# A hand-laid instruction order is replaced by another, and half of the last batch's inverse transform takes its other form

## The chip, the cores and the metric

The kernel runs on one core of a Trainium2 chip. The metric is the device time of one execution in microseconds (us); the kernel before takes 386.0 us, the median of three runs (385.96 to 386.59).

Engine names: PE is TensorE (matrix products), DVE is VectorE, ACT is ScalarE, POOL is GpSimd, SP is SyncE, which here only issues DMAs. Each engine works through its own queue in order; an instruction that waits holds everything behind it.

## The reference, cut to what matters

```python
# attention: batch 4, 8 heads, 768 rows, 64 channels a head, 16 clusters
q_assign = argmax(q_n @ c_n.T);  k_assign = argmax(k_n @ c_n.T)   # per row
mask   = q_assign[:, None] == k_assign[None, :]
attn   = softmax(where(mask, (q @ k.T) / 8, -1e9)) @ v
# then, per batch, on the 768 x 512 matrix x of all heads:
proj = x @ w_proj;  x1, x2, x3 = thirds of proj
conv = irfft(rfft(x2, axis=rows) * rfft(filter, axis=rows))
out  = (x1 * conv * x3) @ w_out
```

## The kernel before

**Attention.** Two heads make a pair; there are 16 pairs, four to a batch. For pair `p` (all names below carry the pair's number):

- four (or eight half) loads bring q and k into the tile `raw`, two loads bring v into `vraw`. There are five `raw` slots (a pair takes two) and three `vraw` slots.
- `tr`: q and k are transposed into `qkT`, for pairs 0 to 2 by PE and a copy, from pair 3 on by two DVE block transposes (L828).
- `cast`: four bf16 copies of it into `aug`, on POOL or ACT.
- `sim`: PE multiplies by the centroids; then `oh`, a chain of DVE steps (L862 to L876) makes the one-hot assignment, and one more step (L900 on ACT, L902 on DVE) scales it. Eight small DMAs, the mask DMAs (L909, 12 KB each, on SP's queue), put it into extra rows of `aug`, so that the scores' product itself carries the mask.
- six steps `sk`, each with `S` (PE, scores into PSUM), `E` (ACT, the exponential of 128x1536 elements into `pb`, L938 or L944), `PV` (PE, into the PSUM tile `outs`, L954), and `acc` (DVE, the running sum of the `pb`, L965).
- `den` (PE) sums `acc` over rows, and a chain follows: an ACT copy (L996), a DMA `dd` to DRAM, a DMA back (`dn`), a DVE reciprocal (L1002), a DMA `dr` out, and two DMAs `rb` that bring it back broadcast. ACT copies `outs` to `osb` (L976); there are two `osb` slots. DVE's step `x` (L1030) multiplies `osb` by `rb` and frees the `osb` slot. PSUM has one `outs`: the next pair's first `PV` waits for this pair's `osb` copy.

**PSUM.** Eight banks: 0 to 2 for scores, 3 and 4 for `outs`, 5 to 7 for everything else. Up to pair 3 a second set of scores may use banks 5 to 7.

**The second part** (`hyena`, one batch at a time, spread among the attention of the next batch): `u` (PE, the x2 projection, split into sum and difference of the halves by DVE), `F` (PE, the forward transform; DVE multiplies by the filter's spectrum `hm`), `G` (PE, x1 and x3, multiplied into the tile x13), `I` (PE, the inverse transform, then times x13 into `y2`), `o` (PE, the product with w_out, a copy, and the store). The letters `I3.0` to `I3.3` are the four channel groups of the last batch. The tables of the transform are made at the start: angles (`ang`), six Sin activations (`sin`), `inv`, and the filter's spectrum (`f`, from the loads `fl`).

**The inverse has two forms.** The direct one: two PE operations, each six products for one half of the rows, and DVE multiplies each half by x13 straight from PSUM (L1119). The butterfly: one PE operation makes an even and an odd part, a copy `od` (ACT or DVE) brings the odd part out of PSUM, DVE adds and subtracts (L1141), and one product with x13 (L1143, DVE or POOL) gives `y2`. Before, the last batch takes the direct form in all four groups, the others the butterfly.

**The order.** `Plan` holds 1564 operations with their dependences; `ORDER` is a written-out list of their numbers in the order in which they are emitted, and so fixes each engine's queue; a letter chooses the engine where two can do it (a: ACT, d: DVE, p: POOL). `Plan.told` follows the list. While it emits, `Plan` keeps a clock of its own, with `LAG` for the time from an operation's end to the release of those that wait for it; that clock decides only which free buffer or PSUM bank a value takes.

Of the kernel before, what the change touches and what calls it, by code (L numbers as in the profile page):

```python
# [29 lines left out]
DIRECT = (3,)  # L30
# [9 lines left out]
0 192 1 9 8 77 47 193 49 78 10 11 263 12 13 79d 14 15 16 17 87p 3 80p 4 5 48 6 7 18 19 35 36 37 38 39 40 41 42 43  # L40
44 45 20 25 26 23 24 55 56a 53 54a 51 52a 46 21 22 61 83d 32 31 88d 30 264 50 84d 29 59a 60a 28 27 57a 58a 34 194
195a 33 198 199a 62 63 64 65 66 67 68 70d 73 75 69 71 72d 76d 196 197a 204 74a 203a 150 151 153 157 200a 104 106
105 103 158 154 201a 255 189 205 89 90d 206 207 208 183 185 182 188 253 186 107 85 209 81 210 202d 211 212d 161 152
162 156 86d 160 164 269 265 267 266a 270a 165 216 184 213 220 187 126 219 259 256 215 108 217 214 260 218 166 155
169 82a 268a 168 170 93 273a 91 95 94 274a 96 92 159 275 272p 2 99 98 163 173 167 171 276 277 278 279 280 281 282
271p 335 221 97 334 283d 111 109 110d 174 340 222 112a 172 224 225 341 342 343 344 345 346 227 228 229 223 232 226
113 233 114a 339a 230 338p 337p 336p 236 237 240 234 241 284 287 285 288 127 291 257 290 289 258 286 254 347 231
235 500 501 124 175 125 329 191 330 176 328 562 324 331 239 128 295 238 292 296 293 348a 327 325 559 354 351 352
355 353 298 242 299 244 506 507 177 508 509 129 243 245 294 311 300 303 304 510 302 511 512 306 513 312 297 504p
130 505p 503p 502p 307 301 308 131 133a 138 139a 349 178 356 493 350 190 261 326 364 365 514a 132a 305 144 180 246  # L50
179 262 310 145a 146a 566 565 181 309 360 361 315 571 357 316 358 567p 572 573 574 575 576 363 577 367 494 491 490
520 517 626 247 492 516 317 522 313 141 372 314 373 569a 359 368 100 570p 140a 369 318 497 496 495 558 515 248 578
319 579a 568a 518 521 249 519 320 586 561 362 366 376 322 321 580 555 587 556 584 557 377 147 370 148a 534 535 374
115 371 375 631 630 379 523 636 142a 524 381 526 382 634p 527 378 134 560 383 637 638 639 323 640 641 136 529 642
380 530 525 528 632a 531 542 135a 633a 543 101 635p 384 333 585 583 533 385 695 696 537 643 119 532 332 581 582 251
538 536 701 539 116a 591 700p 592 540 117 588 702 541 703 386 622 250 625 252 704 387 388 389 589 118a 644a 544 546
595 120a 547 545 596 705 706 594 707 402 400 691 690 564 624 687 685 590 401a 598 403 708 652 688 686 599 143a 600
593 390 650 621 649 404 602 603 597 137a 391a 604 646 651 689 692 620 645 623 548 627 549 395 392 396a 697p 698a
699p 607 601 397 606 394 861 862 608 709a 398 393 399 605 867 648 647 563 716 865p 864p 149a 866a 863p 656 415 868
869 416 657 715 1215 710 499 498 711 855 857 714 712 917 417 870 418 550 611 419 927 871 653 654 612 659 872 918  # L60
551 856 916 613 614 552 553 437 609 610 438 420 660 661 655 405 406 668 446 658 873 628 629 713 669 664 447 665 407
662 926 874 663 615 408 672 667 932 933 409 717 858 666 424 934 554 671 930p 673 875a 928a 421 725 425 726 929a 426
670 412 718 410 674 413 427 411 935 931p 719 721 675 676 422 720 722 677 851 616 880 852 883 876 921 922 881 853
617 854 678 729 723 920 877 879 882 730 414 428 936 724 992 423 937 991 938 429a 733 734 727 450 451 997 737 731
448 735 878 1050 982 618 1212 981 1052 679 1051 859 919 1213 983 1053 431 728 430 939 998 449 732 619 995a 738 996a
940a 903 439 452 435 946 942 440 736 680 993p 904 994a 740 884 885 739 433 741 887 434 886 432p 888 742 891 1214
941 948 860 923 1056 944 947 681 693 743 744 892 436 453 999 890 1057 894 745 694 683 943 746 1000 747 945 682 889
459 461 895 460 896 454 893 899 455a 900 462 898 1001 902 457 1002 897 463 901 956 1062 1060p 464 957 749 1063 684
1064 456 1003 458d 907 949 908 950 905 465 906 952 1059a 953 987 748 985 1049 988 750 466 1004 1005a 1065 1066 467
955 102 1061p 123a 468a 1058a 469 951 758 960 954 961 756 757a 958 909 470 1067 759 760 471p 964 965 986 984 1222  # L70
1047 1223 910 1013 1046 1009 1012 1010 1048 962 1006 1011 1007 1008 798 799 753 968 441 959 911 963 969 966 1025
912 442a 443 967 444 1068 1226a 1026 751 752a 755 754 1069 970 1014 1228 972 445p 1015 971 973 1070a 1229 1230 1231
1232 1233 1283 914 1284 1071 1073 974 1077 1281 975 763 761 762a 1017 765 764 484 1016 1018 485a 486 925 807 768
# [12 lines left out]
489 1365 1118a 1366 1411a 1413 1112 1119 1113d 1331 1121 1120 1368 802 1369 1333 803d 805 804 1122 1372 1114 1332
1334 1367 1115 1371 1123a 1116 1373 806p 1416 1273 1417 1274 1419 1415 1275 848 1124 1126 849a 850 1418 1376 1125
1377 1412 1414 1370 1375 1379 1129 1380 842 1130 843a 1374 1127 1181 1128 1131 1381 1384 1378 1183 1385 1182 1420
1132 1421 1383 1134 1382 1435 1386 844 1335 1336 1276 1133 1388 1436 1135 1337 1136 1389 1387 1139 1423 1424 1137
1140 1422 1427 1138 1426 1141 1428 1425 1155 1156 1431 1429 833 1432 1390 1338 1339 1391 1392 1184 1393 1394 1430  # L90
1434 1438 1340 1395 1439 1187 1433 834a 1440 1442 836 837a 835 838 1341 1396 1185 1186 1188 1189 1437 1190a 1191
1192 1193d 1168 845 1444 1445 1446 1447 1448 1449 839 1441 1172 1174 846a 1450 1169 1443 1451 1173 1175 1466 1170
1171 1176 1177a 1179 1178 1180d 1469 1467 1161 1462 1452 1470 1159 1468a 1160 1163 1472 1162 1471 1164a 1166 1165
1157 1158 1167d 1453 1455 1459 1463 1456 1460 1142 1146 1454a 1458 840a 1461a 1464 1147 1143 1457 1465 1150 1514
1144 1148 1473 1475 1151a 841 847 1152 1145 1153 1149 1490 1494 1518 1520 1154p 1197 1491a 1515a 1495a 1519a 1198a
1516 1517a 1476 1474 1477 1199 1483 1484 1485 1501 1200 1486 1487 1201a 1503 1206 1488 1207a 1489a 1521a 1480 1481
1478 1479 1482 1202 1507 1505 1492 1508a 1502a 1203 1504a 1204a 1506d 1509d 1208 1194 1512 1510 1497 1195a 1493a
# [321 lines left out]
def kernel(  # L421
# [39 lines left out]
    op = P.op  # L461
# [573 lines left out]
    def hyena(b, d0, d1):  # L1035
# [181 lines left out]
```

## Time and profile before

| | |
|---|---|
| median of three runs | 386.0 us (385.96 to 386.59) |
| the profiled execution's own time | 386.6 us |
| its span, first to last instruction | 384.8 us |
| mean granted TensorE clock | 0.988 |
| busy: PE, DVE, ACT, POOL | 364.8, 332.2, 254.0, 58.4 us |
| PE's instructions | 3335 matmuls, all recorded |

Between the span and the execution's own time lie 1.8 us outside the program's instructions. The engines run at the same time, so the busy times do not add up; an engine's idle time costs nothing unless the end of the program waits for it.

A row of the table by stretches reads: from:to and length in us, then busy us and number of instructions of PE, PE's weight loads, DVE, ACT and POOL, then the granted clock, the DMA engines' share and GB/s. A row of the chain reads: start, length, and what ran or was waited for. SPq and DVEq are the sequencers that issue.

### The profile page before, as it was taken

What the parts mean: (1) busy time and instruction counts of PE and PEld (TensorE: products, weight loads), DVE (VectorE), ACT (ScalarE), POOL (GpSimd) and SP (SyncE); (2) the same over time, 40 slices, a digit from 0 to 9 for tenths busy, and PEclk for the clock granted to TensorE, in tenths of its full rate; (3) what the DMA queues carried; (4) which work ended last, traced back from release to release, by engine and by line L of the source; (5) the groups of instructions that cost most, each with busy time, mean ns of one, the idle gap of its engine ahead of it and who ended that gap; (6) DMA issues with size and microseconds to landing.
All of it is one profiled execution on the core that took longest, in us unless ns stands there. A gap on an engine that the chain in (4) does not pass through costs nothing.

```text
span 384.8 us, 8428 instructions
## 1 busy us (share of the span) xinstructions
PE 364.8 (95%) x3335; PEld 188.9 (49%) x3335; DVE 332.2 (86%) x428; ACT 254.0 (66%) x305; POOL 58.4 (15%) x74
## 2 busy tenths in 40 slices
PE   7689897997999999999999999999999999999994
PEld 3243444453444554455444545545454545556662
DVE  7898989796898899799888999998977979887771
ACT  3989985886688676785867764887856555242512
POOL 4005171211202030204013040020101000001000
PEclk9989999999899999999999999999999999999998
DMA  9979594938684664755921435342312003010205
GB/s 179 197 93 170 89 166 86 162 63 139 141 120 81 121 109 85 121 100 112 129 36 40 113 55 119 87 119 46 99 36 75 31 24 119 0 57 29 86 28 191
DMA packets 132289, 37.08 MB, mean 96 GB/s; under 512 B 123485, under 2 KB 125977, under 8 KB 132249
## 3 DMA queue, kind: packets, MB, share of 16 engines
q1 hardware_dynamic: 131000, 34.41, 45.9%
q0 software_dynamic: 1104, 2.10, 3.3%
q8 instruction: 26, 0.43, 0.5%
q14 instruction: 15, 0.11, 0.1%
q10 hardware_dynamic: 144, 0.03, 0.0%
HBM read 30.66 MB, written 6.48 MB: 97 GB/s over the span
## 4 chain that ended last, share of the span: by engine, by line
PE 77%; DVE 7%; DMA 6%; SPq 6%; issue 1%; ACT 1%; DVEq 0%; POOL 0%; POOLq 0%; ACTq 0%
PE outs L954 25%; PE bank L479 22%; PE scores L479 18%; PE outs L479 3%; SPq L909 3%; DMA k<-in_moe_filter_fft_dram 3%; PE bank L986 2%; SPq L541 2%; PE bank L859 2%; PE bank L992 2%; DMA rb<-dr 1%; DMA raw<-in_k_dram 1%; PE bank L745 1%; DVE acc L965 1%; ACT pb L938 1%
## 5 line engine op out<-in xcount | busy, mean ns | idle before, releaser
L938 ACT ACTIVATE pb<-scores 128x1536 f32<-128x1536 f32 x91 | 132.3, 1454 | 56.4 <-PE scores L479 54.2
L954 PE MATMUL outs<-pb,vraw 128*64 128x512 f32 (+1 forms) x768 | 142.9, 494 | 2.3 <-ACT osb L976 2.3
L965 DVE TENSOR_TENSOR acc<-acc,pb 128x1536 f32<-128x1536 f32 x52 | 91.6, 1761 | 2.8 <-ACT pb L938 1.8
L954 PEld LDWEIGHTS outs<-pb,vraw 128*64 128x64 f32 x768 | 55.2, 138 | 71.7 <-issue 59.8
L479 PE MATMUL scores<-aug,aug 128*64 128x256 bf16 (+2 forms) x728 | 76.7, 331 | 7.6 <-ACT pb L938 4.6
L479 PEld LDWEIGHTS <-aug 128*64 128x64 bf16 (+2 forms) x768 | 43.8, 111 | 41.5 <-issue 18.2
L468 POOL CAST aug<-qkT 64x768 bf16<-64x768 f32 x30 | 37.3, 1248 | 163.0 <-PE scores L479 83.1
L479 PE MATMUL bank<-xT,wpj 128*64 128x384 bf16 x384 | 38.1, 326 | 0.0
L479 PEld LDWEIGHTS <-wpj 128*64 128x64 bf16 x512 | 28.9, 110 | 16.2 <-issue 1.2
L1143 POOL TENSOR_TENSOR k<-yy,x 128x768 bf16<-128x768 f32 x7 | 13.0, 1861 | 126.8 <-DVE x L1100 56.6
L479 PEld LDWEIGHTS <-k 128*64 128x64 bf16 (+1 forms) x480 | 23.6, 109 | 17.3 <-issue 4.0
L965 DVE TENSOR_TENSOR acc<-pb,pb 128x1536 f32<-128x1536 f32 x16 | 29.1, 1820 | 0.4 <-ACT pb L938 0.2
L466 ACT CAST aug<-qkT 64x768 bf16<-64x768 f32 x33 | 27.2, 828 | 1.3 <-PE scores L479 0.8
L828 DVE STREAM_TRANSPOSE qkT<-raw 128x768 f32<-128x768 f32 x26 | 24.4, 958 | 2.3 <-DMA rb<-dr 1.7
L1070 DVE TENSOR_TENSOR tm<-bank,hm 128x1024 f32<-128x1024 f32 x18 | 21.6, 1213 | 3.6 <-PE bank L745 2.4
L479 PE MATMUL bank<-wpj,xT 128*64 128x512 bf16 x160 | 20.3, 380 | 0.0
L1030 DVE SCALAR_TENSOR_TENSOR xT<-osb,rb 128x768 bf16<-128x768 f32 x16 | 16.7, 1048 | 3.7 <-DMA rb<-dr 3.4
L479 PE MATMUL bank<-wout,k 128*64 128x512 bf16 x136 | 17.4, 379 | 0.0
L466 ACT COPY os<-bank 128x512 f32<-128x512 f32 x15 | 8.8, 584 | 12.7 <-PE bank L479 11.8
L976 ACT COPY osb<-outs 128x769 f32<-128x769 f32 x16 | 12.8, 798 | 6.0 <-PE outs L954 3.3
L1060 DVE TENSOR_TENSOR k<-bank,us 128x512 bf16<-128x512 f32 x18 | 11.7, 684 | 5.3 <-PE bank L479 2.7
L479 PEld LDWEIGHTS <-xT 128*64 128x64 bf16 x192 | 10.7, 110 | 9.7 <-issue 1.6
(176 smaller groups left out, 408.0 us busy)
## 6 DMA issues: line engine op xcount, KB each, us to landing
vraw<-in_v_dram SPq DMA_DIRECT2D x32, 192.0 KB
rb<-dr SPq DMA_DIRECT2D x30, 192.0 KB
out_dram<-os SPq DMA_DIRECT2D x21, 256.0 KB
raw<-in_q_dram SPq DMA_DIRECT2D x52, 96.0 KB
raw<-in_k_dram SPq DMA_DIRECT2D x52, 96.0 KB
aug<-ohT SPq DMA_DIRECT2D x120, 12.0 KB
k<-in_moe_filter_fft_dram SPq DMA_DIRECT2D x4, 384.0 KB
wpj<-in_moe_w_proj_dram POOLq DMA_DIRECT2D x4, 384.0 KB, 5.0
```

Source lines behind the costliest of these rows:

```text
L466: nc.scalar.copy(o, i)
L468: eng[e].tensor_copy(o, i)
L479: nc.tensor.matmul(out[64 * c:64 * c + 64], lhsT[:, 64 * c:64 * c + 64], rhs, **k)
L828: op("DVE", 0.98, lambda e, j=j: nc.vector.transpose(qkT.t[:, j], raws[p, j].t.rearrange("p t h d -> p (t h d)")), r=[raws[p, j]], w=[(qkT ...
L938: nc.scalar.activation(pb.t[:, :, :S], sps.t.rearrange("p (a b) -> p a b", a=2), Act.Exp, scale=0.125)
L954: nc.tensor.matmul(o.t[64 * hp:64 * hp + 64, lo:hi], vv.t[:, hp, sk], pb.t[:, hp, lo:hi], start=(sk == 0), stop=(sk == NT - 1))
L965: nc.vector.tensor_tensor(acc.t, a, pb.t[:, :, :S], op=Alu.add)
L976: op("ACT", 0.82, lambda e: nc.scalar.copy(osb.t, o.t[:, :S + 1]), r=[o], w=[osb], due=step(i) + 5.0)
L1030: op("DVE", 1.01, lambda e: V.scalar_tensor_tensor(xT.t, osb.t[:, :S], osb.t[:, S:S + 1], rb.t, op0=Alu.add, op1=Alu.mult), r=[osb, rb], w ...
L1060: op("DVE", 0.69, lambda e, m=m, e_=e_, alu=alu, ps=ps, us=us: V.tensor_tensor(uv2()[:, e_, m], ps.t, us.t, op=alu), r=[ps, us], w=[(uv, ( ...
L1070: op("DVE", 1.2, lambda e, i=i, cs=cs, ps=ps, tm=tms[cs]: V.tensor_tensor(tm.t, ps.t.unsqueeze(1).to_broadcast([128, 2, DM]), hm.t[:, i, c ...
L1143: op(("DVE", "POOL"), (0.95, 2.4), lambda e, dt=dt, yt=yt, x13=x13: eng[e].tensor_tensor(y2v()[:, dt], yt(), x13.t.rearrange("p a b -> p ( ...
```

## The change

Four edits:

```diff
-DIRECT = (3,)
+DIRECT = ((3, 2), (3, 3))
...
-    LAG = {"PE": 0.26, "ACT": 0.08, "DVE": 0.08, "POOL": 0.1, "SP": 1.4, "ACTQ": 2.0}
+    LAG = {"PE": 0.26, "ACT": 0.08, "DVE": 0.08, "POOL": 0.1, "SP": 1.8, "ACTQ": 2.0}
...
-            if b in DIRECT:
+            if (b, dt) in DIRECT:
...
-                op("PE", 0.215 * (k1 - k0), f, r=[(y2, (kt, x)) for kt in range(k0, k1) for x in range(1 + (b in DIRECT))] + [wout], w=[ps],
+                op("PE", 0.215 * (k1 - k0), f, r=[(y2, (kt, x)) for kt in range(k0, k1) for x in range(1 + ((b, kt) in DIRECT))] + [wout], w=[ps],
```

and the whole of `ORDER` (1564 entries before, 1566 after) is replaced by a new list:

```diff
-0 192 1 9 8 77 47 193 49 78 10 11 263 12 13 79d 14 15 16 17 87p 3 80p 4 5 48 6 7 18 19 35 36 37 38 39 40 41 42 43
...
-1548 1553 1557 1549 1558d 1550d 1554a 1555 1551 1559
+23 25 26 0 264 24 1 9 35 36 37 38 39 40 41 42 43 44 45 55 46 8 77 78 29 30 31 32 3 2 48 28 27 33 34 10 50 87d 11 12
...
+1547 1548a 1549 1542 1543 1544a 1545 1559 1560d 1561
```

Groups I3.0 and I3.1 take the butterfly, I3.2 and I3.3 keep the direct form. PE's queue has 423 operations for 425, DVE's 423 for 421, ACT's 286 for 291, POOL's 62 for 55, SP's 371 in both. `LAG` for SP goes from 1.4 to 1.8; no instruction waits for it, it only moves the planner's own clock.

The lists in words, at the places that the prediction uses ("place" is the number in that engine's queue, counted from 0):

| queue | before | after |
|---|---|---|
| SP, first mask DMA of pair 1, 2, 3 | places 25, 40, 66 | 21, 48, 65 |
| SP, last mask DMA of pair 1, 2, 3 | 39, 50, 75 | 41, 61, 79 |
| SP, loads of pairs 4 to 6 issued before pair 2's first mask DMA | 5 | 13 |
| pair 3's last one-hot step (`oh3/#5`) | ACT, behind a cast and four `E` of pairs 1 and 2 | DVE, right behind its transpose |
| SP, the two loads of v3 | 56 and 76 | 88 and 93 |
| SP, the two loads of v4 | 77 and 82 | 62 and 76 |
| DVE, `x0`, `x1`, `x2`, `x3` | 98, 133, 118, 135 | 94, 112, 132, 140 |
| SP, `rb` DMAs of pair 1 | 124 and 127 | 106 and 108 |
| ACT, the six `sin` | behind S0's last `E` | between the last two `E` of pair 0 |
| PE, ahead of the first `u` | 33 `S`, 30 `PV`, 8 `sim`, 6 `f` and the rest | 35 `S`, 33 `PV`, 9 `sim`, 5 `f` and the rest |
| four of the last batch's products x1 times x3 | DVE 4 | POOL 3, DVE 1 |
| last PE operation, its copy | `o3.2` second part; two DVE copies in a row | `o3.4` second part; one DVE copy |

Between the fixed places the new list also swaps casts (ACT 33 to 30, POOL 30 to 31, DVE 1 to 3), three steps of the angles to POOL, and the order of the six steps inside a pair.

More of the change, by code (lines that the diff above doesn't have):

```diff
@@ L45 @@
[L45 to L49, printed above, removed]
@@ L100 @@
-1548 1553 1557 1549 1558d 1550d 1554a 1555 1551 1559
+23 25 26 0 264 24 1 9 35 36 37 38 39 40 41 42 43 44 45 55 46 8 77 78 29 30 31 32 3 2 48 28 27 33 34 10 50 87d 11 12
+13 14 15 16 193 192 88p 17 18 49 19 56a 51 52a 53 54a 58a 60a 57a 20 89 90d 263 21 22 61 59d 62 63 64 65 66 67 68
+73 196 197a 198 199a 194 195a 204 202a 69 71 70d 74d 75 72a 76a 161 162 153 154 103 105 106 183 104 203a 157 150
+151 79p 4 83p 5 6 182 186 189 205 200d 206 130 84p 80p 7 207 208 209 210 211 85 212d 201d 81 156 107 158 218 259
@@ new lines @@
+292 295 238 242 296 293 243 244 299 245 509 566 510 511 300 565 512 298 513 302 294 311 297 349 559 496 355 353 126
+350 178 356 352 622 261 354 128 180 351 179 312 620 557 491 621 246 492 303 304 514a 301 357 307 308 305 309 306
+181 360 310 129 495 190 522 517 494 247 191 558 493 518 516 490 358 567p 571 572 248 249 573 515 623 521 562 520
+313 361 568a 314 364 365 117 315 118a 569a 359 570a 316 368 363 574 367 575 631 317 250 519 251 369 576 630 371 577
+556 555 560 318 362 372 373 366 376 377 370 131 523 374 636 375 578 379 252 634a 132a 524 526 133a 579a 527 378 380
@@ new lines @@
+381 637 638 639 640 319 641 529 642 643 530 531 525 119 534 134 528 633p 632p 100 101 635p 382 120a 535 542 141 532
+644a 543 142a 538 539 581 586 561 582 585 583 580 584 320 383 332 533 695 696 651 587 627 384 322 321 625 647 537
+536 699p 385 386 624 701 702 541 591 138 540 700a 135a 592 588 140a 698a 589 333 626 652 388 387 697p 98 703 136
+704 323 861 705 706 862 707 594 544 545 546 599 144 590 600 547 595 596 146a 145a 593 867 603 597 604 708 389 650
+649 548 645 868 395 397 396a 869 870 598 399 607 608 139a 687 648 564 855 549 646 688 690 691 686 692 689 709a 712
@@ new lines @@
+1002 1064 1284 748 981 1222 749 907 905 964 908 906 467 465 951 468a 965 750 1003 1065 466 470 1066 1283 909 910
+986 911 1004 1005a 912 1010 1053 1047 1006 1007 469 1067 955 758 751 752a 956 957 756 954 471p 757a 1013 1009 1011
+1008 1012 1048 1051 960 1223 759 760 961 1068 959 958 807 1228 968 969 962 761 762a 963 1229 1069 1070d 1230 1014
+1077 1076 914 1015 808 966 809 1017 970 967 1231 810 1232 1233 1234 441 1225p 1226p 1227p 1224a 1018 442a 972 444
+1235 443 763 1074 1046 971 1021 1022 445p 753 1016 765 1050 1049 1287 764 754 1020 1024 1025 973 1026 1052 1071 755
@@ new lines @@
+1214 483 813 1100 777 1097 780 1343 814 1102 781 1248 1247 782 1249 783 1252 815 122a 1346a 816a 1253 1101 1041
+1342 784 817 818 1250 1103 1348 1256 1104 1349 1251 1255 785 478 1254 1257 1347a 1344p 1345a 786 1042 1398 819p 484
+1260 796 1258 1105 1106 1107 797 1350 485a 1261 1307 1043 1044 1306 1305 1259 1351 1263 1352 1302 1309 1055 1054
+1108 1110 1109 1264 1265 479a 1262 789 1317 787 790a 792 1045 788 791 1318 1402p 793p 1397 820 1266 1310 800 1353
+801 1268 1267 821 1311 1269 1403 486 1354 1355 1404 1405 1111 1356a 1313 1314 802 472 1312 803a 1406 1407 805 804
@@ new lines @@
+1276 1133 1136 837a 1424 1386 1388 1387 1389 1426 1337 1427 1422 1428 1139 1185 1183 1431 1186 838 1390 1338 1391
+1432 1140 1430 1434 1181 1168 1182 1425 1435 1137 1429 1184 1138 1392 1436 1169 1141 1438 1339 1340 1393 1395 1394
+1439 1440 1442 1433 1189 845 1187 1190a 846a 847 1172 839 840a 841 1444 1192 1341 1191 1445 1396 1446 1188 1447
+1448 1157 1437 848 1449 1193d 1441 1174 1155 1170 1173 849a 850 1156 1443 1450 1451 1175 1176 1171 833 842 1158
+1452 1459 1159 1460 1462 1177a 1178 1179 1180d 1161 1463 834a 1160 1461a 1162 1465 1464 1163 1455 1469 1453 1466
@@ new lines @@
+1456 1470 1142 1467 1164a 843a 1454a 835 1165 1166 1167d 1458 1457 1468a 1143 1471 1144 1145 1472 844 1150 1146
+1151a 1148 1147 1494 1475 1473 1153 1149 1152 1516 1154p 1520 1492 1490 1203 1495a 1204a 1517a 1521a 1476 1474 1477
+1478 1479 1480 1488 1206 1504 1518 1508 1481 1482 1491d 1207a 1493a 1489a 1205 1208 1485 1519d 1486 1483 1484 1487
+1506 1522 1523a 1209 1194 1502 1195a 1503a 1496p 1497 1524p 1509d 1507d 1505d 1210a 1498a 1499 1500 1501d 1525 1527
+1511 1531 1533 1529 1535 1510p 1512a 1526 1528 1513 1211 1196 1200 1514 1532d 1534d 1515d 1540 1536a 1530a 1538
```

80 lines of the change are left out of this document (26 added, 54 removed).

## The prediction

> **What bounds the kernel now.** The first part of the page is read first, then busy time by stretches, because a share over the whole span mixes stages.
>
> ```profile
> span 384.8 us, 8428 instructions
> PE 364.8 (95%) x3335; PEld 188.9 (49%) x3335; DVE 332.2 (86%) x428; ACT 254.0 (66%) x305; POOL 58.4 (15%) x74
> ```
> ```profile
> 0.00:24.00 24.00, 16.18 (x101) 7.97 (x103) 20.41 (x60) 17.34 (x23) 4.67 (x25) 0.93 1.21 174
> 24.00:64.00 40.00, 37.95 (x319) 18.82 (x315) 36.33 (x42) 34.73 (x46) 14.56 (x18) 1.00 0.71 119
> 64.00:72.00 8.00, 5.86 (x54) 3.23 (x58) 5.60 (x6) 5.25 (x8) 0.69 (x1) 1.00 0.95 170
> 72.00:88.00 16.00, 15.66 (x135) 7.89 (x131) 14.97 (x17) 13.08 (x15) 4.51 (x6) 1.00 0.61 89
> 88.00:96.00 8.00, 5.55 (x48) 2.88 (x42) 5.13 (x8) 4.95 (x6) 0.15 (x1) 0.99 0.92 149
> 96.00:104.00 8.00, 7.92 (x55) 3.32 (x52) 6.82 (x8) 5.31 (x6) 1.86 (x3) 0.79 0.55 122
> 104.00:376.00 272.00, 271.91 (x2610) 143.06 (x2608) 241.62 (x289) 171.63 (x203) 31.96 (x23) 1.00 0.37 78
> 360.00:376.00 16.00, 16.00 (x188) 10.48 (x186) 12.36 (x19) 4.42 (x9) 0.00 (x0) 1.00 0.10 35
> 376.00:384.80 8.80, 3.71 (x36) 1.71 (x30) 1.29 (x2) 1.68 (x4) 0.00 (x0) 0.87 0.56 209
> ```
>
> The first busy column is PE. From 104 to 376 us it has work in 271.91 of 272 us at the full clock: there a shorter wait elsewhere buys nothing, and only less PE work counts. Before 104 us it idles 7.82 + 2.05 + 2.14 + 0.34 + 2.45 + 0.08 = 14.9 us, and one stretch runs at a granted clock of 0.79. A microsecond gained there reaches the end undiminished, if DVE (241.62 of 272) keeps up. So the waits are next, first PE's and DVE's, then those of SP's queue, and the chain of work with them.
>
> ```profile
> PE scores L479 <- DMA aug<-ohT: 2.1, 1, 2.1
> PE outs L954 <- ACT osb L976: 2.3, 1, 2.3
> ...
> SPq L909 <- ACT ohT L900: 22.8, 6, 6.3
> SPq L909 <- DVE inv L468: 5.2, 1, 5.2
> ```
> ```profile
> 64.02 1.98 DMA aug<-ohT
> ...
> 86.73 5.71 DMA rb<-dr
> 92.53 1.03 DVE xT L1030
> 93.64 0.81 ACT osb L976
> 94.49 4.07 PE outs L954 x16
> 303.00 1.29 PE outs L954 x8
> ```
> ```profile
> 66.14 0.84 PE L479 MATMUL scores<-aug,aug 80*64 80x512 bf16 x8 [2.15 <-DMA aug<-ohT]
> ```
>
> Three losses can be seen. (a) `S3` stands 2.15 us to 66.14, until the last mask DMA of pair 3 (issued 64.02) has landed. (b) `PV4#0` stands 2.34 us to 94.49: `osb3` had no slot, `x2` frees one, and its `rb` took 5.71 us to land. `x2` is ahead of `x1` on DVE, so neither of the two slots was free. (c) The 16 matrix products behind that wait last 4.07 us; eight take 1.29 us elsewhere, so 4.07 - 2 x 1.29 = 1.49 us goes to the half clock. Together 5.98 us.
>
> **The change part by part: the start.** The loss at (a) has two causes in the old queues.
>
> ```profile
> 43.94 0.57 DVE L876 STREAM_TRANSPOSE ohT<-oh 128x384 bf16<-128x384 bf16 x1
> 52.75 0.71 ACT L900 ACTIVATE ohT<-ohT,mk 128x384 bf16<-128x384 bf16 x1
> ```
> ```profile
> L909 SPq DMA_DIRECT2D aug<-ohT x120: 507/580/1824, 23.1 to 297.7; - x120
> ```
>
> Pair 3's one-hot tile is transposed at 43.94 + 0.57 = 44.51, but its last step runs on ACT at 52.75 to 53.46, 9 us later. And SP stood 5.2 us at place 40, pair 2's first mask, in front of loads that wait for nothing. After, the last step is on DVE right behind the transpose, and 13 loads instead of 5 come ahead of pair 2's masks. Pair 3's last mask moves from place 75 to 79: four more issues of 0.58 us (2.3 us) against 5.2 us not stood, so it is issued at 64.02 + 2.3 - 5.2 = 61.1 by this rough count, at 59.1 when I lay the queue out instruction by instruction with the trace's durations. With 1.98 us to land it is there between 61.1 and 63.1. PE, laid out likewise, reaches `S3` at 61.2; in the old order it was there at 63.99. The wait left is 0 to 1.9 us; I take 0.2, by the finer of the two countings.
>
> At (b), `x1` moves from DVE place 133 to 112 and `x2` from 118 to 132, and with them `rb` of pair 1 goes to SP places 106 and 108. Place 108 was issued at 86.73 before; without the 5.2 us stand that is 81.5. Plus 5.71, 1.03 and 0.81 us, `PV4#0` can start at 89.1, or at 86.3 by the finer laying, where the mask stands and the landings of the long chain of small DMAs fall more favourably. PE gets there between 86.3 (laid) and 90.0 (92.15 less the 2.15 of (a)). The wait left is 0 to 2.8 us; I take 0.8. With that, (c) does not come back; with 2.8 us it would, and cost 1.49 again.
>
> Start-up: 5.98 - 0.2 - 0.8 = 5.0 us gained. Ends: 6.6 us, where the laying puts the first `u` ahead; and 5.98 - 2.8 - 1.49 = 1.7 us, or lower still if DVE decides (rival 2). The reason for caution is DVE: from 24 to 104 us it is busy 36.33 + 5.60 + 14.97 + 5.13 + 6.82 = 68.9 of 80 us. To come 5 us earlier with the same work, its idle time there must shrink from 11.1 to about 6 us.
>
> ```profile
> L965 DVE TENSOR_TENSOR acc<-pb,pb x16: 1744/1750/2379, 23.1 to 314.9; 128x1536 f32<-128x1536 f32 x16
> L468 POOL CAST aug<-qkT x30: 816/825/2397, 29.5 to 262.0; 64x768 bf16<-64x768 f32 x30
> ```
>
> The casts moved from ACT (33 to 30) to DVE (1 to 3) and POOL, and the three angle steps moved to POOL, lie in this stretch too; ACT idled more than DVE in the later part of it, and POOL's 14.56 of 40 us has room. I cost them at nothing; without cover the two casts are about 1.7 us of DVE, by the usual 0.825 us of POOL's, which is inside the gap between 5.0 and 6.6.
>
> [...] The trace has a wait of 2.15 us at 64 with clock 1.00 behind it, and one of 2.34 us at 92 with 0.79 behind it: the shorter shows no dip, the longer does. [...]
>
> **The butterfly in `I3.0` and `I3.1`.**
>
> ```profile
> 110.74 1.73 PE bank L479 x16
> ...
> 188.29 1.10 PE bank L479 x16
> ...
> 369.77 1.95 PE outs L479 x24
> ```
> ```profile
> L1141 DVE TENSOR_TENSOR yy<-bank,od 128x384 f32<-128x384 f32 x20 | 10.8, 551 | 2.4 <-ACT od L466 2.3
> L1143 DVE TENSOR_TENSOR k<-yy,x 128x768 bf16<-128x768 f32 x5 | 4.8, 955 | 0.1
> L1119 DVE TENSOR_TENSOR k<-outs,x 128x384 bf16<-128x384 f32 x4 | 2.1, 554 | 0.6 <-PE outs L479 0.6
> L466 ACT COPY od<-bank 128x384 f32<-128x384 f32 x8 | 3.8, 476 | 2.7 <-PE bank L479 2.6
> L1104 DVE TENSOR_TENSOR x<-x,raw 128x768 f32<-128x768 f32 x4 | 3.8, 954 | 0.2
> L1143 POOL TENSOR_TENSOR k<-yy,x 128x768 bf16<-128x768 f32 x7 | 13.0, 1861 | 126.8 <-DVE x L1100 56.6
> ```
>
> The direct form's two PE operations are the 1.95 us (last row), a butterfly's one is 1.10 (the row before; the first is the first `u`): PE saves 2 x (1.95 - 1.10) = 1.7 us in a stretch where it is busy 16.00 of 16.00. Against that, DVE loses 4 products of 0.554 and gains 4 of 0.551 and 2 of 0.955: +1.9 us; ACT gets 2 copies of 0.476. Between 360 and 376 us DVE is busy 12.36 and ACT 4.42 of 16, and two of four products x1 x3 more than pay for it (3 go to POOL, -2.9 us on DVE; POOL has none at all then). The latency grows: copy, two steps, product, 0.48 + 2 x 0.55 + 0.96 = 2.5 us in place of 0.55. What follows is `I3.2` and `I3.3` in the direct form, 3.9 us of PE work, so the output product that reads `y2` does not wait. Without that cover the cost is up to 2 x (2.5 - 0.55) = 3.9 us, and a product on POOL comes 1.86 - 0.95 = 0.9 us later; so this part is -1.7, with ends -1.7 and +2.2 (all of the cover gone). I take -1.7, by the 3.6 us that DVE idles in 16.
>
> **The end.**
>
> ```profile
> 379.33 0.38 PE L479 MATMUL scores<-wout,k 128*64 128x512 bf16 x2
> 379.59 0.69 DVE L468 COPY os<-outs 128x512 f32<-128x512 f32 x1 [5.32 <-PE outs L479]
> 380.20 0.68 DVE L468 COPY os<-scores 128x512 f32<-128x512 f32 x1
> 380.91 0.81 SPq L1159 DMA_DIRECT2D out_dram<-os  x2
> ```
>
> PE ends at 379.71, the span at 384.8. After, one DVE copy instead of two in a row follows the last PE operation: it starts about 0.1 us behind it instead of 0.49 (-0.4), and one issue instead of two stands before the store (0.81 for two, -0.3 to -0.4). Taken: -0.7, ends 0 and -0.8.
>
> `LAG`: no instruction waits for it. It can change which slot or bank a value takes, and that costs something only where a slot is reused sooner: 0 taken, and any cost falls under rivals 1 to 3.
>
> **Sum.** Span 384.8 - 5.0 - 1.7 - 0.7 = 377.4; with the 1.8 us outside it 379.2, against 386.6 for the profiled execution. That one is the highest of the runs shown (385.96 to 386.59), 0.6 over their median of 386.0. I forecast 379.0 for the median, between 378.6 and 379.2.
>
> **Rivals.**
>
> 1. v3 comes late. Its second load moves from SP place 76 to 93, behind the pair 1 step that waits for a DMA to land. My laying issues it at 67.5 and has `PV3#0` at 71; a landing like `rb`'s 5.71 gives 73.2, a wait of 2.2 us in place of (a), and by (c) a dip of 1.49 with it: 379.0 + 2.2 + 1.5 = 382.7. For it: 0.95 of the DMA engines' time is taken from 64 to 72, and 0.92 from 88 to 96. Against: fewer bytes should be ahead of it, as the masks now stand apart from the loads. Chance 0.13.
>
> 2. DVE becomes the bound, and the new start brings nothing: only butterfly and end remain, 386.0 - 1.7 - 0.7 = 383.6. For it: DVE's idle time must halve, and it can slow down when POOL works: in the rows above the same sum takes 1.75 us, or up to 2.38; POOL has 7 operations more, so at most 7 x 0.63 = 4.4 us more on DVE. Against: the rows' typical values are the undisturbed ones, and the three products stand in the last batch. Chance 0.12. [...]
>
> 3. Slower. SP has one queue, and at places 113 to 125 it holds pair 5's eight masks, which wait for a last one-hot step on ACT. Behind and among them stand pair 2's `dr` (121), a load of v5 (123) and pair 2's `rb` (128, 129). `x2` (DVE place 132) waits for that `rb`; DVE works in order, so the `acc` steps behind it stop, and then `osb4` and `PV5#0` on PE. Each us is lost whole. The old queue stood up to 6.3 us for such a step, and 22.8 us over six of them. It decides from 386.8 - 379.0 = 7.8 us on; with one stand of 6.3 us, a late landing of 5.71 - 1.98 = 3.7 us on top is 10.0, and the (c) dip is then already in it: 389. Against: most of these stands held nobody up, since PE's waits add up to 2 of any length. Chance 0.12.
>
> **How the numbers follow.** Likeliest 0.58 (379.0; by itself 376.5 to 381), rival 1 0.13, rival 2 0.12, no measurable change 0.05 (the start gives back what the end brings), rival 3 0.12. Two runs of this kernel differ by some 0.2%, 0.8 us, and less cannot be told from no change. Faster: 0.58 + 0.13 + 0.12 = 0.83; same 0.05; slower 0.12. The low end takes all 6.6 us and 0.9 more of the uncertain terms: 386.0 - 6.6 - 1.7 - 0.8 = 376.9, set to 376.2 for the median's spread; the high end, 385.0, holds rivals 1 and 2 with a start that costs 1.4.
>
> **What would show it.** `S3` and `PV4#0` without waits over 0.5 us on PE and a granted clock of 1.00 from 88 to 104 prove the start; the first `u` (before: at 110.74) then stands near 109 with 2 `S`, 3 `PV` and one `sim` more ahead of it. SP at place 40 shows no 5.2 us stand. `I3.0` and `I3.1` as 1.10 us operations without idle behind them prove the butterfly; span end less last PE end near 4.4 instead of 5.1 us the end. The forecast is wrong if PE shows a new wait above 2 us before 130 us (named after v3, `rb` or a mask), if DVE is the releaser of `S` or `PV` waits after 104 us, or if PE is no longer full from there to 370.

## The result and the profile after

The new kernel takes 381.56 us (381.13 to 382.95) where the kernel before takes 386.29 (four executions of each): a ratio of 0.9882, 95% interval 0.9852 to 0.9911. On a second chip it was 0.9898 (0.9866 to 0.9930). Both intervals lie below 1: it is faster, as forecast and inside the range, by 4.7 us where 7.0 had been forecast.

The first rows of the page after, and busy time by the same stretches as before (PE, its weight loads, DVE, ACT, POOL, then clock, DMA share, GB/s):

```profile
span 379.6 us, 8411 instructions
PE 363.7 (96%) x3319; PEld 188.1 (50%) x3319; DVE 334.0 (88%) x430; ACT 251.0 (66%) x306; POOL 70.0 (18%) x81
```
```profile
0.00:24.00 24.00, 16.97 (x108) 9.97 (x108) 20.55 (x56) 17.37 (x26) 8.62 (x35) 0.87 1.07 163
24.00:64.00 40.00, 37.32 (x297) 16.74 (x297) 34.42 (x46) 34.69 (x47) 8.85 (x7) 0.95 0.83 135
64.00:72.00 8.00, 7.07 (x58) 3.27 (x59) 6.54 (x5) 5.68 (x8) 0.82 (x1) 1.00 0.96 142
72.00:88.00 16.00, 15.97 (x142) 7.03 (x140) 15.89 (x17) 14.93 (x18) 4.51 (x5) 1.00 0.74 133
88.00:96.00 8.00, 7.85 (x76) 4.86 (x74) 7.90 (x12) 6.44 (x8) 0.00 (x0) 1.00 0.34 68
96.00:104.00 8.00, 8.00 (x72) 3.38 (x68) 7.52 (x10) 7.66 (x8) 3.42 (x3) 1.00 0.77 144
104.00:376.00 272.00, 270.51 (x2584) 142.84 (x2580) 241.20 (x290) 164.26 (x196) 43.73 (x30) 1.00 0.36 81
```

From 72 to 104 us PE is now full and at full clock; before it lost 2.9 us there and ran at 0.79 in the last stretch. But 24 to 64 us is worse than before: 2.68 us of idle time for 2.05, and a clock of 0.95. PE's waits of over 0.3 us from 24 us on (timeline, with the idle time before each and its releaser) and the chain show what stands there:

```profile
37.65 1.09 PE L479 MATMUL scores<-aug,aug 80*64 80x512 bf16 x8 [2.38 <-DMA aug<-ohT]
64.68 0.52 PE L479 MATMUL bank<-aug,aug 128*64 128x256 bf16 x4 [0.75 <-DMA aug<-ohT]
127.85 1.51 PE L954 MATMUL outs<-pb,vraw 128*64 128x512 f32 x8 [0.74 <-DMA vraw<-in_v_dram]
```
```profile
34.37 3.14 DMA aug<-ohT
37.65 1.09 PE scores L479 x8
38.74 2.56 PE outs L954 x8
41.30 0.90 PE bank L986 x8
...
46.22 1.29 PE outs L954 x8
65.19 0.67 PE scores L479 x8
72.60 0.78 PE bank L986 x8
```

`S1#0`, pair 1's first score product, stands 2.38 us for pair 1's last mask (SP place 41, issued 34.37, 3.14 us to land). The three operations behind it run at half clock for most of their time (the granted clock is 0.50 from 38.11 to 41.52 us): 1.09 + 2.56 + 0.90 = 4.55 us for what takes 0.67 + 1.29 + 0.78 = 2.74 further on. So the new order has a loss of 2.4 + 1.8 = 4.2 us at a place where the old one waited 0.97 us. Both sides had moved: PE comes to it at 35.27 us, in the old order at 38.88, and the mask leaves SP at 34.37 instead of 32.63. About 1 us of the wait is not the mask's: in two runs below whose masks left earlier (*new_sp*, *new_pool*), `S1#0` still waits 1.04 us, for `pb`.

The end of the span, to set against the two DVE copies in a row of before:

```profile
374.01 1.25 PE L479 MATMUL bank<-wout,k 128*64 128x512 bf16 x10
375.30 0.69 DVE L468 COPY os<-bank 128x512 f32<-128x512 f32 x1 [1.90 <-PE bank L479]
375.74 0.81 SPq L1159 DMA_DIRECT2D out_dram<-os  x2
```

PE ends at 375.26, 4.45 us earlier than before (379.71); behind it come 4.34 us instead of 5.09. The span's 5.2 us are thus 4.45 in PE's time and 0.75 at the end. The run *i_direct* below takes 1.46 of the 4.45 as the butterfly's; 3.0 are left. Up to 104 us PE idles 10.8 us instead of 14.9, and the half clock costs 1.8 instead of 1.5: that is 3.7 us for the start, where 5.0 had been taken. A new wait of 0.74 us behind it, at `PV6#0` (the last row of the waits), takes the rest back.

### The profile page after: what moved, and what is told of

Read it like the earlier page. It is cut to its first block, busy times and chain, and to the rows that moved or that the text cites. A ratio compares the mean times of both kernels' runs of the same rounds, so it can differ in the third digit from the quotient of the medians.

```text
span 379.6 us, 8411 instructions
## 1 busy us (share of the span) xinstructions
PE 363.7 (96%) x3319; PEld 188.1 (50%) x3319; DVE 334.0 (88%) x430; ACT 251.0 (66%) x306; POOL 70.0 (18%) x81
## 4 chain that ended last, share of the span: by engine, by line
PE 74%; SPq 7%; DVE 6%; DMA 5%; ACT 5%; issue 2%; POOL 0%; POOLq 0%; DVEq 0%; ACTq 0%
PE outs L954 24%; PE bank L479 22%; PE scores L479 17%; SPq L541 4%; DMA aug<-ohT 3%; SPq L909 3%; PE outs L479 3%; PE bank L986 2%; DMA vraw<-in_v_dram 2%; ACT pb L938 2%; PE bank L992 2%; DVE acc L965 2%; PE bank L859 1%; PE bank L745 1%; ACT pb L944 1%
## 5 line engine op out<-in xcount | busy, mean ns | idle before, releaser
L938 ACT ACTIVATE pb<-scores 128x1536 f32<-128x1536 f32 x88 | 127.9, 1453 | 53.5 <-PE scores L479 51.1
L965 DVE TENSOR_TENSOR acc<-acc,pb 128x1536 f32<-128x1536 f32 x52 | 94.0, 1807 | 4.0 <-ACT pb L938 3.1
L479 PE MATMUL scores<-aug,aug 80*64 80x512 bf16 (+2 forms) x704 | 74.8, 330 | 5.1 <-DMA aug<-ohT 2.4
L468 POOL CAST aug<-qkT 64x768 bf16<-64x768 f32 x31 | 39.2, 1273 | 175.9 <-PE scores L479 106.5
L479 PE MATMUL bank<-xT,wpj 128*64 128x384 bf16 x368 | 36.5, 326 | 0.0
L479 PEld LDWEIGHTS <-k 128*64 128x64 bf16 (+1 forms) x464 | 21.6, 109 | 18.7 <-issue 5.8
L466 ACT CAST aug<-qkT 64x768 bf16<-64x768 f32 x30 | 24.5, 829 | 0.5
L976 ACT COPY osb<-outs 128x769 f32<-128x769 f32 x16 | 12.8, 802 | 10.9 <-PE outs L954 10.8
L479 PE MATMUL bank<-inv,k 128*64 128x384 bf16 (+1 forms) x196 | 18.1, 330 | 0.0
L1073 DVE TENSOR_TENSOR k<-tm,tm 128x1024 bf16<-128x1024 f32 x12 | 15.5, 1290 | 0.2
L1100 DVE TENSOR_TENSOR x<-bank,x 128x384 f32<-128x384 f32 x20 | 10.9, 544 | 4.3 <-PE bank L479 4.2
```

What stands on the lines that cost most here:

```text
L466: nc.scalar.copy(o, i)
L468: eng[e].tensor_copy(o, i)
L479: nc.tensor.matmul(out[64 * c:64 * c + 64], lhsT[:, 64 * c:64 * c + 64], rhs, **k)
L938: nc.scalar.activation(pb.t[:, :, :S], sps.t.rearrange("p (a b) -> p a b", a=2), Act.Exp, scale=0.125)
L965: nc.vector.tensor_tensor(acc.t, a, pb.t[:, :, :S], op=Alu.add)
L976: op("ACT", 0.82, lambda e: nc.scalar.copy(osb.t, o.t[:, :S + 1]), r=[o], w=[osb], due=step(i) + 5.0)
```

## The experiments

Times are compared with the kernel before, run on the same chip; 0.01 is 3.9 us. A place is the number in SP's queue. In the lists of that queue, l5 is one of the loads of pair 5's q and k, v2 one of the two loads of pair 2's v, fl one of the filter's; dn, dr and rb are the small DMAs of the chain behind `den`.

**masks1_early**: pair 1's masks ahead of the loads between them.

```diff
 SP from place 21 (mN: pair 1's mask N)
-m5 l4 m1 l3 l3 l3 l3 m7 m2 l5 l5 fl l5 l5 m6 l4 v2 m3 m4 l4 m0
+m5 m1 m7 m2 m6 m3 m4 m0 l4 l3 l3 l3 l3 l5 l5 fl l5 l5 l4 v2 l4
```


> The new order, with pair 1's eight mask DMAs issued in a row at SP places 21 to 28 (the loads between them go behind). In the new kernel S1#0 stands 2.4 us for the last of these masks, issued at 34.37 from place 41, and the PE work behind it runs at half clock (PV0#5 2.83 us, den0 1.61). Theory A (that wait and the half clock behind it are what the new start loses): S1#0 starts near 35.3, no half clock behind it, PE 4 us earlier there, and 3 us or more of it reach the end: about 378.5. Theory B (SP's queue is the bound of the start: it issues without a break, and pair 3's last mask still leaves from place 79 at about 61.8): the wait comes back at S3 and grows there from 0.75 to about 4 us; 0 to 1.5 us reach the end: 380.0 to 381.6. Theory C (DVE is the bound): as B, but S or PV wait for acc or pb instead of a mask.

Measured 0.9980 (0.9955 to 1.0005): the whole gain was gone. The last mask left at 26.2 and nobody waited for it any more, but PE stood elsewhere, first at `sim3`, with half clock again, and DVE in front of it for a load of l3:

```profile
33.39 2.35 PE L859 MATMUL bank<-qkT,cbd 128*32 128x384 f32 x8 [2.60 <-DVE qkT L828]
55.66 0.84 PE L479 MATMUL scores<-aug,aug 80*64 80x512 bf16 x8 [2.00 <-DMA aug<-ohT]
69.64 0.52 PE L479 MATMUL bank<-aug,aug 128*64 128x256 bf16 x4 [2.20 <-DMA aug<-ohT]
```
```profile
32.36 1.84 DVE L828 STREAM_TRANSPOSE qkT<-raw 128x768 f32<-128x768 f32 x2 [3.73 <-DMA raw<-in_k_dram]
```

None of the three theories had foreseen that: the loads of pair 3 that now stood behind the masks are used at 28.9 us in the new kernel, by a transpose on DVE. S2 and S3 then waited for masks too; for S3 theory B had said so.

**masks1_3_early**: the same, and pair 3's masks in a row.

```diff
 SP from place 62 (nN: pair 3's mask N)
-v4 fl l5 n0 l7 l6 n6 n4 fl n1 dr n7 n3 l8 v4 n5 rb n2
+n0 n6 n4 n1 n7 n3 n5 n2 v4 fl l5 dr l7 l6 fl l8 v4 rb
```


> As the run before, and pair 3's eight masks in a row at SP places 62 to 69 instead of 65 to 79, pair 0's dr after the loads behind them. Theory A and B both: no wait at S1 and none over 0.5 us at S3; 3.5 to 4.5 us faster than the new kernel, 377 to 378. Theory C (DVE): the gain stops at about 1.5 us, 380, with PE's waits named after acc or pb, or v3, v4 or an rb that stand behind the masks become the new wait (each us late is lost).

Measured 1.0040 (1.0014 to 1.0066), slower than before, where theories A and B had both given 377 to 378 us. The l3 loads were late as in the last run. A load of pair 5's q, now behind the masks (place 64 to 72), held DVE for 6.33 us, and PE stood 3.14 us at 70.08 for the `pb` behind it:

```profile
65.40 0.98 DVE L828 STREAM_TRANSPOSE qkT<-raw 128x768 f32<-128x768 f32 x1 [6.33 <-DMA raw<-in_q_dram]
```

Both runs point one way: this queue has hardly an entry that can wait, so bringing one forward makes another late.

**pe_filled**: products of no use in PE's 2.4 us at S1.

```diff
-inv1 inv2 S1#0
+inv1 warm warm warm warm warm inv2 S1#0
```


> The new order with five products of no use (64 columns by 512, 0.43 us each) on PE in the 2.4 us in which S1#0 stands for its mask. S1#0 starts no earlier (37.65). If PE's idle time there is what brings the half clock behind it, S1#0, PV0#5 and den0 run at their usual 0.65, 1.29 and 0.78 us and the end comes 1.5 us earlier (380.0), or less where the next mask takes it back. If the half clock has another cause, PV0#5 stays at 2.8 us and the time at 381.5.

Measured 0.9900 (0.9868 to 0.9932), the new kernel's own ratio. The half clock is gone (first fence the run, second the new kernel), so it was PE's idle time that had brought it:

```profile
36.00:40.00 4.00, 3.99 (x39) 1.79 (x39) 3.97 (x6) 4.00 (x6) 3.29 (x3) 1.00 0.94 149
40.00:44.00 4.00, 4.00 (x42) 2.09 (x36) 3.65 (x6) 3.58 (x7) 0.00 (x0) 1.00 0.96 152
```
```profile
36.00:40.00 4.00, 2.35 (x12) 1.23 (x14) 3.97 (x6) 2.94 (x5) 2.85 (x2) 0.76 1.12 150
40.00:44.00 4.00, 4.00 (x34) 1.49 (x32) 2.11 (x4) 2.11 (x5) 0.00 (x0) 0.81 0.95 153
```

The five products took 1.27 us together, 0.25 each and not 0.43. PE was 2.3 us ahead at `sim4` (47.76 for 50.04; 0.64 of that already at `S1#0`, which started at 37.01), and gave it back at pair 3's mask, with 1.97 us of wait instead of 0.75:

```profile
64.17 0.52 PE L479 MATMUL bank<-aug,aug 128*64 128x256 bf16 x4 [1.97 <-DMA aug<-ohT]
```

0.5 us of lead is left behind it. That mask left SP at 61.2, in the new kernel at 61.8 (first fence this run, second the new kernel): SP hardly comes earlier because PE does. This is theory B's mechanism.

```profile
61.20 0.59 SPq L909 DMA_DIRECT2D aug<-ohT  x1
```
```profile
61.79 0.59 SPq L909 DMA_DIRECT2D aug<-ohT  x1
```

**i_direct**: the new order with the direct form in all four groups.

```diff
-DIRECT = ((3, 2), (3, 3))
+DIRECT = ((3, 0), (3, 1), (3, 2), (3, 3))
```


> The new order with all four channel groups of the last batch in the direct form again: I3.0 and I3.1 are two PE operations of 0.975 us each instead of one of 1.10. If the butterfly is worth what PE saves, the time rises by 1.7 us against the new kernel (383.3). If its longer chain (copy, two steps, product) had cost part of it, the rise is smaller, down to none.

Measured 0.9914 (0.9887 to 0.9942), too near 0.9882 and 0.9898 for the times to decide. The traces do. From the operation ahead of `I3.0` (first line of each fence) to PE's last one (last line), by the chain, here *i_direct* and then the new kernel:

```profile
360.07 0.65 PE scores L479 x8
360.73 0.97 PE outs L479 x12
361.70 1.95 PE scores L479 x24
...
377.81 0.23 PE outs L479 x2
```
```profile
358.76 0.81 PE scores L479 x10
...
374.17 1.10 PE bank L479 x10
```

377.81 + 0.23 - 360.07 = 17.97 us with the direct form, 374.17 + 1.10 - 358.76 = 16.51 in the new kernel: 1.46 us for two butterflies. No wait of PE is in either stretch.

**new_again**: the new kernel itself, on the chip of the next three.

> The new kernel itself, as the reference for the other runs of this chip: about 0.988 of the kernel before.

Measured 0.9898; its S1 waited 2.53 us, its S3 1.27. *i_direct*, whose start is the same list, waited 3.76 and 0.56 us there: one trace gives such a wait to about 1 us only. The 1.97 us of *pe_filled* at S3 lies above all three.

**new_sp**: pair 1's last four masks ahead of loads that are due later than l3, six late loads behind pair 3's masks.

```diff
-... m7 m2 l5 l5 fl l5 l5 m6 l4 v2 m3 m4 l4 m0
+... m7 m2 m6 m3 m4 m0 l5 l5 fl l5 l5 l4 v2 l4
-l6 ... v4 fl l5 n0 l7 l6 n6 n4 fl n1 dr n7 n3 l8 v4 n5 rb n2 rb
+... fl l5 n0 n6 n4 fl n1 dr n7 n3 n5 rb n2 rb l7 l6 v4 v4 l6 l8
```


> The new order; pair 1's last four masks go ahead of the loads of pair 5, the filter and v2 (the last mask at SP place 33 instead of 41), but stay behind pair 3's loads; and six loads that are not needed before 76 us (of l6, l7, l8 and v4) go behind pair 3's masks, whose last one moves from place 79 to 73. Theory B of the runs before (SP's queue, in which every entry costs about 0.57 us, sets the start, and an entry may only be put back if nobody waits for it): the wait at S1#0 and the half clock behind it go (4.0 us), and S3's last mask leaves at least 6 x 0.57 = 3.4 us earlier, so that 2 to 3.5 us reach the end: 378 to 379.5 where the new kernel takes 381.5. Theory C (DVE, with acc and the one-hot steps, is the bound): under 1 us, with PE's waits named after pb, acc or qkT.

Measured 1.0015 (0.9985 to 1.0045): the gain gone again, where theory B had given 378 to 379.5 us. S1 waits 1.04 us without half clock and S3 not at all, as meant. But l4 comes late (its last load leaves at 40.4 instead of 37.9) and holds `sim4`, with half clock, and then v3 holds `PV3#0` (its second load leaves at 75.28 instead of 70.63):

```profile
50.82 1.51 PE L859 MATMUL bank<-qkT,cbd 128*32 128x384 f32 x8 [2.74 <-DVE qkT L828]
78.50 1.07 PE L954 MATMUL outs<-pb,vraw 128*64 128x512 f32 x4 [2.01 <-DMA vraw<-in_v_dram]
```

**old_a** and **old_ab**: the two places of the prediction mended in the old order.

```diff
 (a)
-oh3/T2 (DVE) ... oh3/#5 (ACT, behind four E)
+oh3/T2 (DVE) oh3/#5 (DVE)
-SP 40: pair 2's masks, fl l4 l4 l4 fl fl among and behind them
+SP 40: fl l4 l4 l4 fl fl, then pair 2's masks
-SP 59: l5 l7 l5 l5 l5 l5 l7, then pair 3's masks
+SP 59: pair 3's masks, then l5 l7 l5 l5 l5 l5 l7
 (b)
-SP: dn of pair 1 at 89, dr at 102, rb at 124 and 127; DVE: x2, ..., x1
+SP: dn at 83, dr at 90, rb at 95 and 96; DVE: x1, ..., x2
```


> Part (a) of the run before alone. Theory of the prediction: 2.15 us less, 384.2. Rival: PV4#0 waits for the rb of pair 2 whenever PE gets there, so the wait there grows by what (a) brings, and the time stays at 386.3; or half of it, since SP no longer stands 5.2 us and issues that rb earlier.

> The old order with the two places mended that the prediction names. (a): pair 3's last one-hot step on DVE right behind its transpose, six loads ahead of pair 2's masks, pair 3's masks ahead of eight loads. (b): pair 1's dn, dr and rb earlier on SP, x1 ahead of x2 on DVE. Theory of the prediction: S3 and PV4#0 do not wait and no half clock follows; 2.15 + 2.34 + 1.49 = 6.0 us at most, 5.0 taken: 381. Theory B (SP's queue): the waits move to the entries that were put back, and less than 2 us reach the end.

Measured: (a) 0.9943 (0.9914 to 0.9973), 2.2 us; (a) and (b) 0.9964 (0.9941 to 0.9987), 1.4 us. The longest wait that is left, first with (a) alone, then with both:

```profile
91.81 2.80 PE L954 MATMUL outs<-pb,vraw 128*64 128x512 f32 x16 [2.19 <-ACT osb L976]
```
```profile
84.69 1.49 PE L479 MATMUL scores<-aug,aug 80*64 80x512 bf16 x8 [2.66 <-DMA aug<-ohT]
```

(a) is worth what the prediction said, though the interval is wide (1.0 to 3.3 us), and its rival is out: PE comes to `PV4#0` 2.5 us earlier and still waits only 2.19, since SP, which no longer stands 5.2 us, issues the `rb` earlier too (84.25 for 86.73). No half clock follows this time. (b) takes the wait at `PV4#0` away and puts one of 2.66 us at `S4`: pair 1's small DMAs had been put ahead of pair 4's masks. That is theory B again, against the 381 us of the prediction's theory.

**new_pool**: seven large loads issued by POOL.

```diff
-fl#0 fl#1 fl#2 fl#3 v2#1 v4#0 v4#1 on SP
+the same entries of the list with the letter p (POOL)
```


> The new order with nothing put back: seven large loads (the filter's four, v2's second, v4's two) are issued by POOL, whose queue idles most of that time, instead of SP. Each stays at its place in the list. Two of them stand ahead of pair 1's last mask on SP (0.72 + 1.47 us there), five more ahead of pair 3's (3.0 us). Theory B (SP's queue, one entry after another, sets the start): S1's last mask leaves 2 us earlier, its wait falls under 0.5 us with no half clock behind it, S3's last mask leaves 4 to 5 us earlier; 3 to 4 us less than the new kernel: 378. Rival D (not the queue but the landings: the DMA engines are over 1.0 busy from 30 to 40 us, and a mask that leaves earlier lands as late as before): S1 keeps over 1.5 us of wait; under 1 us gained. Rival E (loads issued by POOL land later, or hold POOL's casts): PE's waits are named after qkT, aug casts or k; no gain or a loss of 1 to 3 us.

Measured 0.9967 (0.9946 to 0.9988). S1 behaves nearly as theory B says (under 0.5 us given): 1.04 us of wait, named after `pb`, and no half clock. Then, where five POOL loads run, a single mask's issue takes 4.5 us on SP, pair 0's `dn` lands late, DVE stands 6 us for it in order, and PE with it:

```profile
L909 SPq DMA_DIRECT2D aug<-ohT x120: 507/576/4538, 21.3 to 300.6; - x120
```
```profile
55.00 0.23 DVE L1002 RECIPROCAL dn<-dn 128x12 f32<-128x12 f32 x1 [6.04 <-DMA dn<-dd]
```
```profile
55.42 1.49 PE L479 MATMUL scores<-aug,aug 80*64 80x512 bf16 x8 [5.93 <-DMA aug<-ohT]
```

**old_a_fly**: (a), the butterfly, and another engine for one copy at the end, in the old order. The four products x1 times x3 of the last batch stay on DVE, where the new kernel has three of them on POOL.

> The old order with part (a) mended, the butterfly in I3.0 and I3.1, and one DVE copy instead of two behind the last PE operation. Part (a) alone measured 0.9943 of the kernel before (2.2 us). If the three add up: 2.2 + 1.5 to 1.7 + 0.3 to 0.7 = 4.0 to 4.6 us, 381.8 to 382.4, the new kernel's time without its order. If the longer chain of the butterfly is not covered in the old order: I3.3 and the o3 products wait, and less than 1 us comes on top of (a), 383.5.

Measured 0.9942 (0.9911 to 0.9973), no better than (a) alone. In this order the output products wait for `y2`:

```profile
374.50 1.27 PE L479 MATMUL scores<-wout,k 128*64 128x512 bf16 x10 [1.58 <-DVE k L1119]
```

This 1.58 us is as much as the butterfly's 1.5. The releaser is the last product of DVE, which is busy 9.86 of the 10.4 us before. So two things can be behind the wait, and no run parts them: the old order has no other PE work there to cover the longer chain, and DVE has the three products that the new kernel gives to POOL. Nor did the end come out as the new kernel's: two DVE copies still follow each other (379.05 and 379.66), and 4.9 us lie behind PE's last operation, for 5.1 before and 4.3 in the new kernel. The profiled execution took 386.15 us, above the median of 383.56: it waits 2.90 us at S1 and 3.38 us at `PV4#0`, where *old_a* waits 0.97 and 2.19. These waits lie 280 us ahead of the end.

**two_pool** and **two_pool_s3**: only the two loads that POOL can issue at 11 us go to POOL; in the second, three late loads (l7, l8, v4) also go behind pair 3's masks.

> The new order, and of the seven loads that POOL issued in the run before only two, the filter's second and v2's second: POOL issued them at 10.7 and 11.6 us, well ahead of pair 1's masks; the five that it issued at 38.8 to 49.7 us, beside a mask whose issue took 4.5 us, are on SP again. Theory F (S1's mask is late by SP's queue, and the loss in the run before came from the loads issued together around 40 us): S1#0 waits 1.0 us with no half clock (2.4 us and 1.5 us of half clock in the new kernel), S3's last mask leaves 2 us earlier, no 6 us wait at S2; 2 to 2.8 us less than the new kernel, ratio to the kernel before 0.982 to 0.984. Theory G (the six dn, dd, rb and mask DMAs land late whatever the queue does): S2 or S3 wait again by what S1 gained; ratio 0.988 to 0.992.

> As the run before, and three loads that nothing reads before 88 us (of l7, l8 and v4) go behind pair 3's last mask and pair 0's rb, whose places in the queue become 74 and 75 instead of 77 and 78 (1.7 us). Theory F: what wait S3 still has (0.75 us in the new kernel, up to 1.5 us when PE comes earlier) goes, 0.5 to 1.5 us less than the run before: 0.979 to 0.982. Theory G: no difference to the run before beyond 0.5 us, or a new wait at PV3#0 or PV4#0 for v3 or v4.

Measured 0.9854 (0.9824 to 0.9884) and 0.9894 (0.9869 to 0.9919). In the first, the waits at S1, S2 and S3 are

```profile
35.56 0.84 PE L479 MATMUL scores<-aug,aug 80*64 80x512 bf16 x8 [0.61 <-ACT pb L938]
50.12 0.84 PE L479 MATMUL scores<-aug,aug 80*64 80x512 bf16 x8 [1.44 <-DMA aug<-ohT]
63.21 0.52 PE L479 MATMUL bank<-aug,aug 128*64 128x256 bf16 x4 [1.30 <-DMA aug<-ohT]
```

with a clock of 1.00 from 24 us on and a span of 377.3 us, 2.3 less than the new kernel's. But this execution, 379.06 us, is the fastest of six; their median is 380.85. By the ratios the gain over the new kernel is 1.1 us (1.7 against its second chip), between what theories F and G had given. It is the lowest ratio of all runs, but the intervals overlap, and the two were not timed on one chip, so a gain is not shown. What the trace shows is where the 4.2 us of S1 went: the wait fell to 0.61 and the half clock went, and S2 and S3 wait 2.0 us more than in the new kernel. In the second run S3 does not wait, but half clock follows S1 (a wait of 1.04 us there, one of 0.69 just before), and `PV3#0` waits for v3:

```profile
74.31 1.07 PE L954 MATMUL outs<-pb,vraw 128*64 128x512 f32 x4 [2.44 <-DMA vraw<-in_v_dram]
```

## Why the prediction was right, and where a size was off

- **Bound.** Right: behind 104 us PE is busy to its end at 375.26 but for the 0.74 us at `PV6#0`, and the gain came from the start, from less PE work, and from the end.
- **Start: 3.7 us for 5.0, the term that was mis-sized.** The three losses that it named shrank by 5.2 us: S3's wait to 0.75 us (0.2 taken, 0 to 1.9 given), PV4's to nothing (0.8 taken), the half clock behind PV4 to nothing. The step that failed is the one that the text does not have: `S1#0`. The sum takes losses away and asks only at the two old places what comes next; pair 1's last mask, moved from place 39 to 41 behind loads of pair 5, became the new wait, 1.4 us longer than the old one, and with 1.8 us of half clock behind it. "(c) does not come back" failed with it. That is 3.2 us against the sum. 1.7 us came back from idle time that the prediction does not name (0.8 in the first 24 us, 0.9 in short waits up to 104): that the start still brought 3.7 is in part luck.
- **S3's wait is small for another reason than the one given.** Pair 3's last mask left at 61.8, near the rough count of 61.1 and not the finer 59.1, and took 2.84 us to land instead of 1.98: it was there at 64.6, and the prediction had it there between 61.1 and 63.1. The wait is only 0.75 us because PE, held at S1, came at 63.9 and not at the 61.2 laid out. Where PE comes earlier, in *pe_filled* and *two_pool*, the wait grows to 1.97 and 1.30 us.
- **The prediction's own signs.** It called itself wrong if PE showed a new wait above 2 us before 130 us, named after a mask. There is one, at `S1#0`. S3 waits 0.75 us, over the 0.5 that was to prove the start, and the first `u` stands at 112.55 us and not near 109. So the time came out inside the range although the layout of the start was wrong. The other signs held: no wait at `PV4#0`, a clock of 1.00 from 88 to 104 us, no stand of 5.2 us on SP at place 40, the butterflies without idle time, 4.3 us behind PE's end.
- **What held the start.** The caution was put on DVE. DVE does hand waits on, but in the runs its long stands were for DMAs (a load of l3, l4 or l5, a `dn`). The trace of *pe_filled* shows SP's queue as what S3 waits for. Five other kernels brought entries forward or put others back, and in each another entry became the wait (l3, l5, l4, v3, pair 4's masks). Taking two entries off the queue, at a time when the loads disturbed nobody, left PE less idle in the one trace.
- **Butterfly.** 1.46 us for 1.7. The row of 1.10 us for 16 products is too short: by the difference an operation takes 1.95 - 0.73 = 1.22. The rest of it is in the row of the operation behind (0.77 us in the chain where 0.65 is usual). The cover held in the new order; *old_a_fly* has 1.58 us of wait, out of the 3.9 given for no cover at all, though DVE's extra products may be its cause.
- **The end.** 0.75 us for 0.7.
- **Rivals.** v3 late did not happen in the new kernel (its near relative did, 0.74 us for v6), but did in *new_sp*, 2.0 us, where the load left 4.6 us later, and in *two_pool_s3*, 2.4 us, where PE came 3.2 us earlier. Without the half clock it was priced right (2.2). Rival 2, that the new start brings nothing, did not come about, nor did DVE become the bound: it has 7.7 us of idle time left from 24 to 104 us. But only 0.7 of that lies behind 72 us, where DVE is as full as PE, and whether it could follow a still earlier start was not tried. The slowing beside POOL is in both traces: every sum over 1.76 us (6 before, 10 after, of 68) overlaps a POOL instruction, and none without one takes longer; why is not shown. But the median sum still takes 1.75 us with seven more POOL instructions; only the longest grew, from 2.38 to 3.13 us (row by line, ns, shortest, median, longest):

```profile
L965 DVE TENSOR_TENSOR acc<-pb,pb x16: 1740/1750/3132, 22.4 to 306.6; 128x1536 f32<-128x1536 f32 x16
```

- **Rival 3**, the slower one, did not show at its place, but its mechanism, one SP queue whose entries hold each other up, is the one behind S1 and S3.
- **The half clock.** The prediction went by two waits, 2.15 us with none behind it and 2.34 us with row (c) behind it, and took the half clock out of the sum. It did stay in: it moved with PE's wait to S1, and *pe_filled* shows it gone when that wait of 2.38 us is filled. See the last section.

## What to carry to other kernels

When a hand-made order is exchanged, losses that vanish are only half the sum: walk the bound engine's whole queue and ask at each operation what it now waits for, above all for small transfers behind large ones in one queue. A queue in which every entry is due within a few us cannot be mended by swapping entries; take entries off it (here that helped in the trace; in the time it is not clear of the noise), and where they go, look at what runs beside them. A longer chain that costs nothing in one order (the butterfly's copy and sums) can cost all of its gain in another, where PE has nothing else to do or the engine of the chain is full.

## What the runs showed of the hardware

- **Half clock behind a wait.** Over these fourteen traces PE has 13 waits of 2.34 us or more behind 24 us; half clock follows 11 of them (2.34, 2.38, 2.42, 2.53, 2.60, 2.66, 2.74, 2.90, 3.38, 3.76 and 5.93 us), at 1.5 to 1.8 us a time where I summed it. Not behind 3.14 and 2.44 us. Of 20 waits between 0.95 and 2.20 us one has it, 1.04 us with another of 0.69 us just before. So in these traces a wait that grows from 2.2 to 2.4 us mostly costs some 1.7 us more, and not 0.2. The granted clock is 0.50 for 3.41 us behind the wait of 2.34 us (95.87 to 99.29, kernel before) and behind that of 2.38 us (38.11 to 41.52, new kernel).
- **An issue can stall.** A mask's issue on SP takes 0.58 us, but up to 1.82 before and 4.54 us in *new_pool*, the latter between 43.1 and 50.0 us, where POOL issues five loads from 38.8 to 50.6. The cause of the stall was not tried.
